# Regrouping the attention work between the steps of a feed-forward stage: four head pairs in one phase, one phase per step

## The chip, the core and the metric

The kernel runs on one core of a Trainium2 chip. The core has TensorE (PE: matrix products, whose weight loads are shown as PEld), VectorE (DVE), ScalarE (ACT), GpSimd (POOL) and SyncE (SP, which here only issues transfers). Each engine works through its own instruction stream in order; semaphores join them. The metric is the device time of one execution in microseconds, the median of several runs.

## The reference

Two stages follow each other: a linear-attention recurrence over 768 time steps, for 4 batches and 8 heads of width 48, and a feed-forward stage over the 3072 resulting rows of width 384.

```python
for t in range(S):                                    # B, H, S, D = 4, 8, 768, 48
    kt, vt, rt, wt = (k[:, :, t], v[:, :, t], r[:, :, t], w[:, :, t])
    cur = np.einsum('bhd,bhe->bhde', u[None] * kt, vt)
    y[:, :, t] = np.einsum('bhd,bhde->bhe', rt, state + cur)
    state = wt[:, :, :, None] * state + np.einsum('bhd,bhe->bhde', kt, vt)
...
x = attn_out.transpose(0, 2, 1, 3).reshape(B * S, H * D)
h = x @ w_in                                          # 384 x 2048
g = h - np.tanh(h)
return (g @ w_out).astype(np.float32)                 # 2048 x 384
```

All inputs but the weights are float32. The two weight matrices arrive as 64-bit floats and are turned into 32-bit ones on the chip, from their two 32-bit halves.

## The kernel before

**Blocks.** The work is cut into 8 blocks (4 batches, 2 stretches of 384 time steps, `NB`). A block's attention yields `xT`, the transposed 384 x 384 input of its feed-forward stage. That stage has 16 steps (`NF`): step `f` multiplies `xT` with 128 columns of w_in into `hp` (`first`, L374), ScalarE and VectorE form g from it (six operations L381 to L386, five L389 to L396), and two steps later (`LAG`) g is multiplied with w_out and added up in three accumulators `acc` (`Second.add`, L410). The attention of block i+1 runs between the steps of block i; block 0's attention runs ahead of everything ("boot"), and the last block's steps have none beside them. After the last step three tiles `o` are copied from `acc` and stored (L414, L416).

**Attention.** 64 time steps form a chunk, and two heads, one on partitions 0 to 47 and one on 64 to 111, form a pair. `scores` holds, for each pair of time steps of a chunk, how much of the later one's result comes from the earlier one. It is filled level by level: a first product of `kmix` and `rmix` (L222, masked into `scores` at L229), and then for m = 2, 4, 8, 16, 32 a product of `kq` and `rp` of half the width (masked in at L239; for 32 copied by ScalarE at L245). Between the levels `rp` and `kq` are multiplied by products of the decays w: rp on VectorE (L257), kq on GpSimd (L259), and the products `tot` themselves are formed on VectorE (L262). Then kq is transposed (L279, copied to `ks` at L281), multiplied with v (L296), and VectorE carries the states through the chunks (L303). Last come the products of rp with the states (L317) and, behind a fence, of v with the scores (L333), copied to `xT` by ScalarE (L344); the fourth pair goes to `late`, from which six small transfers fill the free partitions of `xT` (L352).

**What sets the order.** A `unit` is a generator that does this for two of the four pairs (`UP = 2`), and yields after each piece. A block has two units (g = 0, 1) that take turns, 20 pieces in all. The main loop asks for `PHASES * NG * (f + 1) / (NF - 1)` pieces by step f, so one step has one piece and the next may have two. TensorE's stream follows the program; those of the other engines are ordered by the scheduler from its own costs. All attention products use one PSUM tile `att` (pool `ps_a`, one buffer of two banks), so a piece's products wait until the products before have been read. Input tiles are double-buffered (`inp`, `once`), v_sb too.

**Weights.** `load_weights(f)` turns one tile of 128 x 768 weights: ScalarE takes the low half (`up`, L164) and the magnitude of the high half (L165), VectorE clamps (L166), takes the sign (L168), shifts (L169) and combines (L171), and GpSimd adds `up` (L173) as 32-bit integers. Three tiles are turned in boot, the others during block 0.

Of the kernel before, what the change touches and what calls it, by code (L numbers as in the profile page):

```python
# [34 lines left out]
F32 = mybir.dt.float32  # L36
# [10 lines left out]
P = 128  # L47
# [7 lines left out]
NG = NPAIR // UP  # L55
# [8 lines left out]
PHASES = 10  # L64
# [11 lines left out]
LOWEST = float(np.array(896 << 20, np.int32).view(np.float32))  # L76
HIGHEST = float(np.array(1151 << 20, np.int32).view(np.float32))
# [3 lines left out]
def kernel(  # L81
# [13 lines left out]
    inp = ctx.enter_context(tc.tile_pool(name="inp", bufs=2))  # L95
    once = ctx.enter_context(tc.tile_pool(name="once", bufs=2))
# [32 lines left out]
    for m in (2, 4, 8, 16):  # L129
        make_mask(m, m, 0)  # L130
# [3 lines left out]
    scores = []  # L134


    states = []
    for i in range(2):
        a = const.tile([P, 2, UP, NCP, L], F32, name=f"scores{i}", tag=f"scores{i}")
        nc.vector.memset(a, 0.0)  # L140
        scores.append(a)
    for g in range(NG):
        row = []
        for q in range(NQ):
            st = const.tile([P, UP, NCH, L], F32, name=f"states{g}{q}", tag=f"states{g}{q}")
            nc.gpsimd.memset(st, 0.0)
            row.append(st)
        states.append(row)
# [3 lines left out]
    w_out_sb = w_sb[:, :, DM:2 * DM]  # L152

# [3 lines left out]
    def load_weights(f):  # L157
        raw = conv.tile([P, 2 * DM, 2], I32, name="raw", tag="raw")
        nc.gpsimd.dma_start(out=raw, in_=weights[f].bitcast(I32).rearrange("p (n two) -> p n two", two=2))
        lo, hi = raw[:, :, 0], raw[:, :, 1]  # L160
        a = conv.tile([P, 2 * DM], I32, name="a", tag="a")
        sign = conv.tile([P, 2 * DM], I32, name="sign", tag="sign")
# [5 lines left out]
        nc.vector.tensor_single_scalar(sign, hi, -2 ** 31, op=ALU.bitwise_and)  # L168
        nc.vector.tensor_scalar(out=a, in0=a, scalar1=1 << 27, scalar2=4,  # L169
                                op0=ALU.bitwise_xor, op1=ALU.logical_shift_left)  # L170
        nc.vector.scalar_tensor_tensor(out=a, in0=a, scalar=1, in1=sign,  # L171
                                       op0=ALU.logical_shift_right, op1=ALU.bitwise_or)
        nc.gpsimd.tensor_tensor(out=w_sb[:, f, :].bitcast(I32), in0=a, in1=up, op=ALU.add)  # L173
# [4 lines left out]
    def unit(b, q, g, ps, v_sb, xT, late):  # L178


        A, St = scores[g], states[g][q]
        cols = slice(q * NB, (q + 1) * NB)
        pairs = slice(UP * g, UP * (g + 1))

        def load(pool, name, src):
            t = pool.tile([P, UC], F32, name=name, tag=name)
            nc.sync.dma_start(out=t.rearrange("d (p t) -> d p t", p=UP),
                              in_=src[b, pairs, :, cols].rearrange("p d t -> d p t"))
            return t


        rmix = load(once, "rmix", rT)
        kmix = load(once, "kmix", kT)
        rp = load(inp, "rp", rT)
        kq = load(inp, "kq", kT)
        wt = load(inp, "wt", wT)
        for p in range(UP):
            for t, odd in ((rmix, 0), (kmix, 1)):
                part = t[:, p * NB:(p + 1) * NB].rearrange("d (n two) -> d n two", two=2)[:, :, odd]
                nc.scalar.activation(out=part, in_=part, func=AF.Copy,  # L200
                                     scale=u_sb[:, UP * g + p:UP * g + p + 1])

        def new_ps():
            return ps.tile([P, 2, BANK], F32, name="att", tag="att")

        def gram(lhs, rhs, m, width):

            n = NCP * UP * width
            ps_t = new_ps()
            gr = ps_t[:, :, 0:n].rearrange("s h (p c t) -> s h p c t", p=UP, c=NCP)  # L210
            for p in range(UP):
                for c in range(NCP):
                    for h in range(2):
                        for par in range(2):
# [3 lines left out]
                            dst = gr[64 * par:64 * par + 64, h, p, c, :]  # L218
# [5 lines left out]
            return ps_t[:, :, 0:n]  # L224

        def take(gr, m):
            if m == 1:
                mask = masks[1].bitcast(U8).rearrange("s b j -> s (b j)").unsqueeze(1).unsqueeze(1)
                nc.vector.copy_predicated(  # L229
                    out=A.rearrange("s h p c t -> s h (p c) t"),  # L230
                    mask=mask.to_broadcast([P, 2, UP * NCP, L]),
                    data=gr.rearrange("s h (n t) -> s h n t", t=L))
                return
            nb = L // (2 * m)
            for h in range(2):
                dst = A[:, h].rearrange("s p c (b two m) -> s (p c) b two m", two=2, m=m)[:, :, :, 1, :]
                src = gr[:, h].rearrange("s (n b m) -> s n b m", b=nb, m=m)
                mask = masks[m].bitcast(U8).unsqueeze(1).to_broadcast([P, UP * NCP, nb, m])
                nc.vector.copy_predicated(out=dst, mask=mask, data=src)  # L239

        def take_top(gr):

            for par in range(2):
                rows = slice(64 * par, 64 * par + 32)
                nc.scalar.copy(out=A[rows].rearrange("s h p c t -> s h (p c) t")[:, :, :, 32:],  # L245
                               in_=gr[rows].rearrange("s h (n t) -> s h n t", t=32))

        take(gram(kmix, rmix, 1, L), 1)
        tot = wt
        m = 1  # L250
        while True:
            nblk = UC // (2 * m)
            t2 = tot.rearrange("d (n two) -> d n two", two=2)
            left, right = t2[:, :, 0], t2[:, :, 1]
            rv = rp.rearrange("d (n two m) -> d n two m", two=2, m=m)[:, :, 1, :]
            kv = kq.rearrange("d (n two m) -> d n two m", two=2, m=m)[:, :, 0, :]
            nc.vector.tensor_tensor(out=rv, in0=rv, op=ALU.mult,  # L257
                                    in1=left.unsqueeze(2).to_broadcast([P, nblk, m]))
            nc.gpsimd.tensor_tensor(out=kv, in0=kv, op=ALU.mult,  # L259
                                    in1=right.unsqueeze(2).to_broadcast([P, nblk, m]))  # L260
            nxt = work.tile([P, nblk], F32, name=f"tot{2 * m}", tag=f"tot{2 * m}")
            nc.vector.tensor_tensor(out=nxt, in0=left, in1=right, op=ALU.mult)  # L262
            tot = nxt
            m *= 2
            yield
            if m == L:
                break
            gr = gram(kq, rp, m, L // 2)
            if m == L // 2:
                take_top(gr)  # L270
            else:
                take(gr, m)


        ks = work.tile([P, UP, NCP, P], F32, name="ks", tag="ks")
        tp = new_ps()
        for p in range(UP):
            for c in range(NCP):
                nc.tensor.transpose(tp[:, p, c * P:(c + 1) * P],  # L279
                                    kq[:, p * NB + c * P:p * NB + (c + 1) * P], ident)  # L280
        nc.scalar.copy(out=ks.rearrange("t p c d -> t p (c d)"), in_=tp[:, :, 0:NCP * P])  # L281
        yield


        last = q == NQ - 1
        kvp = new_ps()
        for p in range(UP):
            for c in range(NCP):
                for h in range(2):
                    for par in range(2):  # L290
                        if last and 2 * c + par == NCH - 1:
                            continue
                        toks = slice(64 * par, 64 * par + 64)
                        e0 = (UP * g + p) * D2 + h * D
                        n0 = (p * NCP + c) * D
                        nc.tensor.matmul(kvp[64 * h:64 * h + 64, par, n0:n0 + D],  # L296
                                         lhsT=ks[toks, p, c, 64 * h:64 * h + 64],
                                         rhs=v_sb[toks, c, e0:e0 + D], start=True, stop=True)
        for c in range(NCH - 1 if last else NCH):
            for p in range(UP):  # L300
                dst = St[:, p, c + 1, 0:D] if c + 1 < NCH else states[g][q + 1][:, p, 0, 0:D]
# [192 lines left out]
```

## Time and profile before

| | us |
|---|---|
| median of 3 runs (904.54 to 908.07) | 907.02 |
| the profiled execution | 905.4 |
| its span, first to last instruction | 903.7 |
| TensorE busy | 736.0 (81%) |
| VectorE busy | 585.3 (65%) |
| ScalarE busy | 474.0 (52%) |
| GpSimd busy | 145.3 (16%) |
| matrix products of the feed-forward stage (acc, hp), busy | 322.5 + 278.4 |
| mean granted clock of TensorE, as a share of full speed | 0.923 |

Line numbers (L222) are those of the listing above. "a<-b,c" reads: a is written from b and c. Every float32 product appears as two records, so a step's six products are 12 records, and a piece of 24 products has 48. A wait is put down to what released it last. A TensorE record's duration includes some of the next one's time, as the products overlap; starts are the better clock.

### The profile page before, as it was taken

What the parts mean: (1) busy time and instruction counts of PE and PEld (TensorE: products, weight loads), DVE (VectorE), ACT (ScalarE), POOL (GpSimd) and SP (SyncE); (2) the same over time, 40 slices, a digit from 0 to 9 for tenths busy, and PEclk for the clock granted to TensorE, in tenths of its full rate; (3) what the DMA queues carried; (4) which work ended last, traced back from release to release, by engine and by line L of the source; (5) the groups of instructions that cost most, each with busy time, mean ns of one, the idle gap of its engine ahead of it and who ended that gap; (6) DMA issues with size and microseconds to landing.
All of it is one profiled execution on the core that took longest, in us unless ns stands there. A gap on an engine that the chain in (4) does not pass through costs nothing.

```text
span 903.7 us, 20566 instructions
## 1 busy us (share of the span) xinstructions
PE 736.0 (81%) x8480; PEld 458.7 (51%) x8480; DVE 585.3 (65%) x1221; ACT 474.0 (52%) x969; POOL 145.3 (16%) x163
## 2 busy tenths in 40 slices
PE   1664768888888888887888888888888888798997
PEld 1652445545555555554555555555555555455554
DVE  2999999647764576647746466554766466654674
ACT  2437356555464644546355453646545454545775
POOL 6555334001110011101110011100111001100000
PEclk9986789999999999999999888999999999999999
DMA  9476221140012300232011310113001100000000
GB/s 330 147 240 211 73 78 61 39 136 28 2 36 76 117 10 1 54 86 97 2 36 37 103 63 1 36 54 122 27 2 36 37 33 1 1 1 7 27 0 27
DMA packets 32493, 55.98 MB, mean 62 GB/s; under 512 B 2960, under 2 KB 30352, under 8 KB 32400
## 3 DMA queue, kind: packets, MB, share of 16 engines
q1 hardware_dynamic: 30096, 42.09, 14.8%
q0 software_dynamic: 2304, 12.58, 3.9%
q8 instruction: 67, 1.10, 0.5%
q14 instruction: 26, 0.21, 0.1%
HBM read 48.76 MB, written 4.72 MB: 59 GB/s over the span
## 4 chain that ended last, share of the span: by engine, by line
PE 58%; DVE 16%; ACT 12%; issue 5%; SPq 2%; DMA 2%; PEld 0%; PEldq 0%; DVEq 0%; ACTq 0%
PE acc L410 27%; PE hp L374 22%; PE att L222 5%; DVE hs L389 4%; PE att L317 3%; ACT s L382 3%; ACT h L381 3%; SPq L352 2%; DVE scores L239 2%; DVE hs L391 2%; DVE states L303 2%; DMA xT<-late 1%; ACT qa L383 1%; DVE gT L396 1%; ACT qb L384 1%
## 5 line engine op out<-in xcount | busy, mean ns | idle before, releaser
L410 PE MATMUL acc<-w_sb,gT 128*128 128x384 f32 x768 | 322.5, 563 | 1.3 <-ACT o L414 1.1
L374 PE MATMUL hp<-xT,w_sb 128*128 128x384 f32 x768 | 278.4, 496 | 9.7 <-DMA xT<-late 9.7
L389 DVE SCALAR_TENSOR_TENSOR hs<-h,s 128x384 f32<-128x384 f32 x128 | 106.5, 832 | 213.1 <-ACT s L382 212.8
L381 ACT COPY h<-hp 128x384 f32<-128x384 f32 x128 | 61.3, 479 | 343.9 <-PE hp L374 343.9
L374 PEld LDWEIGHTS hp<-xT,w_sb 128*128 128x128 f32 x768 | 150.7, 198 | 124.9 <-issue 22.4
L410 PEld LDWEIGHTS acc<-w_sb,gT 128*128 128x128 f32 x768 | 154.1, 212 | 98.0 <-issue 29.2
L259 POOL TENSOR_TENSOR kq<-kq,tot 128x384 f32<-128x384 f32 x80 | 74.2, 927 | 538.2 <-PE att L222 496.4
L222 PE MATMUL att<-rp,kq 48*64 48x32 f32 x3840 | 79.5, 232 | 66.5 <-DVE scores L239 54.9
L222 PEld LDWEIGHTS att<-rp,kq 48*64 48x64 f32 x3840 | 71.4, 148 | 98.9 <-issue 96.1
L396 DVE COPY_PREDICATED gT<-big,th 128x384 f32<-128x384 int32 x128 | 76.8, 600 | 7.4 <-DVE scores L239 0.2
L383 ACT ACTIVATE qa<-s,shift 128x384 f32<-128x384 f32 x128 | 76.9, 601 | 0.0
L384 ACT ACTIVATE qb<-s,shift 128x384 f32<-128x384 f32 x128 | 76.8, 600 | 0.0
L386 ACT ACTIVATE big<-s,shift 128x384 f32<-128x384 f32 x128 | 76.8, 600 | 0.0
L395 DVE TENSOR_TENSOR th<-h,th 128x384 f32<-128x384 f32 x128 | 76.7, 599 | 0.0
L393 DVE SCALAR_TENSOR_TENSOR gT<-qb,hs 128x384 f32<-128x384 f32 x128 | 71.6, 559 | 7.5 <-ACT big L386 0.5
L391 DVE SCALAR_TENSOR_TENSOR hs<-qa,hs 128x384 f32<-128x384 f32 x128 | 70.5, 550 | 0.0
L382 ACT ACTIVATE s<-h 128x384 f32<-128x384 f32 x128 | 66.8, 522 | 3.8
L239 DVE COPY_PREDICATED scores<-mask,att 128x192 f32<-128x192 uint8 x128 | 49.1, 410 | 26.3 <-PE att L222 26.1
L385 ACT ACTIVATE th<-h 128x384 f32<-128x384 f32 x128 | 64.9, 507 | 0.0
L317 PE MATMUL att<-rp,states 48*64 48x64 f32 x768 | 31.9, 246 | 20.0 <-ACT xT L344 19.6
L257 DVE TENSOR_TENSOR rp<-rp,tot 128x384 f32<-128x384 f32 x80 | 48.1, 601 | 0.0
L222 PE MATMUL att<-rmix,kmix 48*64 48x64 f32 x768 | 18.1, 252 | 32.9 <-DVE scores L229 21.1
(42 smaller groups left out, 460.2 us busy)
## 6 DMA issues: line engine op xcount, KB each, us to landing
raw<-in_weights POOLq DMA_DIRECT2D x16, 768.0 KB, 4.6
rmix<-in_rT SPq DMA_DIRECT2D x16, 384.0 KB, 3.3
kmix<-in_kT SPq DMA_DIRECT2D x16, 384.0 KB, 4.0
rp<-in_rT SPq DMA_DIRECT2D x16, 384.0 KB, 3.1
kq<-in_kT SPq DMA_DIRECT2D x16, 384.0 KB, 3.2
wt<-in_wT SPq DMA_DIRECT2D x16, 384.0 KB, 3.2
v_sb<-in_v SPq DMA_DIRECT2D x8, 576.0 KB, 4.0
out_y<-o SPq DMA_DIRECT2D x24, 192.0 KB, 1.9
```

The lines of the kernel that those rows point to most:

```text
L222: nc.tensor.matmul(dst, lhsT=lhs[rows, t0:t0 + L], rhs=src, start=True, stop=True)
L374: nc.tensor.matmul(hp, lhsT=w_in_sb[:, f, kc, :], rhs=xT[:, kc, :], start=(kc == 0), stop=(kc == KC - 1))
L381: nc.scalar.copy(out=h, in_=hp)
L382: nc.scalar.activation(out=s, in_=h, func=AF.Square)
L383: nc.scalar.activation(out=qa, in_=s, func=AF.Square, bias=shift[:, 0:1])
L384: nc.scalar.activation(out=qb, in_=s, func=AF.Square, bias=shift[:, 1:2])
L386: nc.scalar.activation(out=big, in_=s, func=AF.Relu, bias=shift[:, 2:3])
L389: nc.vector.scalar_tensor_tensor(out=hs, in0=h, scalar=SERIES, in1=s, op0=ALU.mult, op1=ALU.mult)
L391: nc.vector.scalar_tensor_tensor(out=hs, in0=qa, scalar=QUAD[0][1], in1=hs, op0=ALU.add, op1=ALU.mult)
L395: nc.vector.tensor_tensor(out=th, in0=h, in1=th, op=ALU.subtract)
L396: nc.vector.copy_predicated(out=g, mask=big.bitcast(I32), data=th)
L410: nc.tensor.matmul(acc, lhsT=g[:, j * P:(j + 1) * P], rhs=w_out_sb[:, f, :], start=(f == 0), stop=(f == NF - 1))
```

## The change

- The class `Block` takes the place of `unit`. Tiles hold all four pairs, twice as wide, and are single (`inp`, bufs=1); they are loaded by `load_all`, asked for at step 14 of the block before the one in whose steps they are used, so each load waits for the tile's last reader.
- A score phase handles all four pairs in one product group (48 products in one `att` tile); the first level and what follows the levels stay in halves. That makes 14 phases (`PHASES`), and the main loop takes one per feed-forward step, f = 0 to 13. The result's two product groups stand together in one phase.
- The multiplications of kq stand on VectorE (`decay`), not on GpSimd.
- Weights: ScalarE scales the magnitude by 2**-48 as it takes it, so that VectorE's shift left by 3 does what the exclusive-or and two shifts did; VectorE also adds `up`, and combines the sign straight into w_sb. GpSimd only issues the loads. Five tiles are turned in boot, one more per step after.
- Boot (`start`) loads k, r, w once per half, takes rmix and kmix from them (VectorE copies half of each, ScalarE scales the other half), and makes four masks and zeroes the states after the first products.
- The stores of out_y are issued by ScalarE, not SP.

```diff
-        nc.scalar.activation(out=a.bitcast(F32), in_=hi.bitcast(F32), func=AF.Abs)
+        nc.scalar.activation(out=a.bitcast(F32), in_=hi.bitcast(F32), func=AF.Abs, scale=SCALE)
...
-        nc.vector.tensor_single_scalar(sign, hi, -2 ** 31, op=ALU.bitwise_and)
-        nc.vector.tensor_scalar(out=a, in0=a, scalar1=1 << 27, scalar2=4,
-                                op0=ALU.bitwise_xor, op1=ALU.logical_shift_left)
-        nc.vector.scalar_tensor_tensor(out=a, in0=a, scalar=1, in1=sign,
-                                       op0=ALU.logical_shift_right, op1=ALU.bitwise_or)
-        nc.gpsimd.tensor_tensor(out=w_sb[:, f, :].bitcast(I32), in0=a, in1=up, op=ALU.add)
+        nc.vector.tensor_single_scalar(a, a, 3, op=ALU.logical_shift_left)
+        nc.vector.tensor_tensor(out=a, in0=a, in1=up, op=ALU.add)
+        nc.vector.scalar_tensor_tensor(out=w_sb[:, f, :].bitcast(I32), in0=hi, scalar=-2 ** 31, in1=a,
+                                       op0=ALU.bitwise_and, op1=ALU.bitwise_or)
...
+        def decay(self, m, p0, n):
+            cols = slice(p0 * NB, (p0 + n) * NB)
+            tot = self.tiles["wt"][:, cols] if m == 1 else self.tots[m, p0]
...
+            for t, half, by in ((self.tiles["kq"], 0, right), (self.tiles["rp"], 1, left)):
+                part = t[:, cols].rearrange("d (n two m) -> d n two m", two=2, m=m)[:, :, half, :]
+                nc.vector.tensor_tensor(out=part, in0=part, op=ALU.mult,
+                                        in1=by.unsqueeze(2).to_broadcast([P, nblk, m]))
...
+        def load_all(self):
+            for name, src in (("rmix", rT), ("kmix", kT), ("wt", wT), ("kq", kT), ("rp", rT)):
+                self.load(name, src, 0, NPAIR)
+            self.load_v()
+        def phases(self, ps):
+            self.mix(0, NPAIR, False)
+            for p0 in (0, UP):
+                self.level_1(ps, p0)
+                yield
+            m = 1
+            while m < L:
+                self.decay(m, 0, NPAIR)
+                m *= 2
+                if m < L:
+                    self.level(ps, m, 0, NPAIR)
+                    yield
+            for p0 in (0, UP):
+                self.turn(ps, p0)
+                yield
+                self.update(ps, p0, True)
+                yield
+            for p0 in (0, UP):
+                self.result(ps, p0)
+                yield
+            self.fill_holes()
+            yield
...
-                    nc.sync.dma_start(out=out[r0:r0 + P, :], in_=o)
+                    nc.scalar.dma_start(out=out[r0:r0 + P, :], in_=o)
...
-                while done < PHASES * NG * (f + 1) / (NF - 1):
-                    done += 1
-                    if next(run, True):
-                        break
+                next(run, None)
+                if f == PHASES and i + 2 < len(blocks):
+                    blocks[i + 2].load_all()
```

TensorE's stream before, within the score levels of a block (one line is a group of equal products; x24 is one unit's half block, x48 two of them in a row). Two steps with one piece, and one with two:

```order
L374 MATMUL hp<-xT,w_sb 128x384 x3
L222 MATMUL att<-rp,kq 64x32 x24
L410 MATMUL acc_2188<-w_sb,gT 128x384
L410 MATMUL acc_2189<-w_sb,gT 128x384
L410 MATMUL acc_2190<-w_sb,gT 128x384
L374 MATMUL hp<-xT,w_sb 128x384 x3
L222 MATMUL att<-rp,kq 64x32 x48
L410 MATMUL acc_2188<-w_sb,gT 128x384
```

The same place after:

```order
L414 MATMUL hp<-xT,w_sb 128x384 x3
L220 MATMUL att<-rp,kq 64x32 x48
L450 MATMUL acc_2068<-w_sb,gT 128x384
L450 MATMUL acc_2069<-w_sb,gT 128x384
L450 MATMUL acc_2070<-w_sb,gT 128x384
L414 MATMUL hp<-xT,w_sb 128x384 x3
L220 MATMUL att<-rp,kq 64x32 x48
L450 MATMUL acc_2068<-w_sb,gT 128x384
```

Before, an x48 row is two groups that write `att` one after the other; after, it is one group in one `att` tile, and every level's step looks alike.

VectorE's stream before, around one step of the levels (hs, th, gT are the dense operations; scores the masked copies; rp the products):

```order
L389 SCALAR_TENSOR_TENSOR hs<-h,s 128x384
L395 TENSOR_TENSOR th<-h,th 128x384
L239 COPY_PREDICATED scores_120<-mask_102,att 128x48x4
L391 SCALAR_TENSOR_TENSOR hs<-qa,hs 128x384
L239 COPY_PREDICATED scores_120<-mask_102,att 128x48x4
L393 SCALAR_TENSOR_TENSOR gT<-qb,hs 128x384
L257 TENSOR_TENSOR rp<-rp,tot_3154 128x96x4
L396 COPY_PREDICATED gT<-big,th 128x384
```

And after, at the level m = 16:

```order
L429 SCALAR_TENSOR_TENSOR hs<-h,s 128x384
L435 TENSOR_TENSOR th<-h,th 128x384
L431 SCALAR_TENSOR_TENSOR hs<-qa,hs 128x384
L263 COPY_PREDICATED scores<-mask_200,att 128x24x16
L433 SCALAR_TENSOR_TENSOR gT<-qb,hs 128x384
L263 COPY_PREDICATED scores<-mask_200,att 128x24x16
L436 COPY_PREDICATED gT<-big,th 128x384
L241 TENSOR_TENSOR kq<-kq,tot_0_4_2261 128x48x16
L241 TENSOR_TENSOR rp<-rp,tot_0_4_2261 128x48x16
```

The copies and products are twice as wide, and the two products of the next level stand behind all five dense operations of the step.

SP's stream after, for one block (before, each of rmix, kmix, kq, rp and wt had two loads of half the width, and the six fills stood behind the loads of wt and v too):

```order
L175 DMA wt<-in_wT 128x4x384
L175 DMA rmix<-in_rT 128x4x384
L175 DMA kmix<-in_kT 128x4x384
L175 DMA kq<-in_kT 128x4x384
L175 DMA rp<-in_rT 128x4x384
L182 DMA v_sb<-in_v 128x3x384
L347 DMA xT<-late 16x384 x6
```

The next block's wt now stands behind the fills, and rp and v ahead of them.

More of the change, by code (lines that the diff above doesn't have):

```diff
@@ L128 @@
     make_mask(1, 2, 1)
[L129 to L148, printed above, removed]
+    A = const.tile([P, 2, NPAIR, NCP, L], F32, name="scores", tag="scores")
+    nc.vector.memset(A, 0.0)
+    states = [const.tile([P, NPAIR, NCH, L], F32, name=f"states{q}", tag=f"states{q}")
+              for q in range(NQ)]
     w_sb = const.tile([P, NF, 2 * DM], F32, name="w_sb", tag="w_sb")
@@ L176 @@
-    fence, fences = tc.alloc_semaphore("fence"), []
[L178 to L211, printed above, removed]
@@ L241, in take_top, with level_1 @@
[L241 to L252, printed above, removed]
+            return used
+        def level_1(self, ps, p0):
+            gr = self.gram(ps, self.tiles["kmix"], self.tiles["rmix"], p0, UP, 1, L)
+            mask = masks[1].bitcast(U8).rearrange("s b j -> s (b j)").unsqueeze(1).unsqueeze(1)
+            nc.vector.copy_predicated(
+                out=A[:, :, p0:p0 + UP].rearrange("s h p c t -> s h (p c) t"),
+                mask=mask.to_broadcast([P, 2, UP * NCP, L]),
+                data=gr.rearrange("s h (n t) -> s h n t", t=L))
@@ L275, in unit @@
[L275 to L298, printed above, removed]
```

303 lines of the change are left out of this document (185 added, 118 removed).

## The prediction

> **What bounds the kernel now.** I read the busy times by stage first: block 0, one block in the middle, and the last one, cut where TensorE starts the first `hp` product of a block (columns: stretch, PE, PEld, DVE, ACT, POOL busy, granted clock, DMA share, GB/s).
>
> ```profile
> 64.20:191.20 127.00, 94.21 (x1041) 58.20 (x1042) 108.80 (x192) 69.17 (x132) 41.53 (x33) 0.82 0.31 101
> 191.20:297.30 106.10, 90.22 (x1069) 55.37 (x1068) 65.25 (x147) 55.71 (x118) 11.46 (x12) 0.94 0.17 51
> 830.10:903.70 73.60, 66.88 (x205) 38.23 (x203) 44.32 (x84) 50.71 (x105) 0.00 (x0) 0.99 0.05 18
> ```
>
> Three regimes: 64.2 us of boot attention, a block 0 in which VectorE is busy 109 of 127 us (it converts weights), six steady blocks of (830.1-191.2)/6 = 106.5 us in which TensorE is the busiest but idles 15.9 us each and has a granted clock of 0.94, and a last block of 73.6 us without attention. Then the waits of TensorE (us in total, times, longest):
>
> ```profile
> PE att L222 <- DVE scores L239: 54.9, 16, 6.9
> PE att L279 <- ACT ks L281: 22.2, 7, 3.2
> PE att L222 <- DVE scores L229: 21.1, 7, 7.6
> PE att L317 <- ACT xT L344: 19.6, 7, 2.8
> PE hp L374 <- DMA xT<-late: 9.7, 9, 6.2
> PE att L296 <- DVE states L303: 5.3, 7, 1.2
> ```
>
> All but the hole fills (xT<-late) and the state updates happen where two attention units follow each other in one feed-forward step and share the one `att` buffer: the second waits until DVE or ACT has read the first one's products. The timeline of PE shows what each costs (start, duration, idle before):
>
> ```profile
> 415.74 0.90 PE L222 MATMUL att<-rp,kq 48*64 48x32 f32 x48
> 416.57 2.20 PE L410 MATMUL acc<-w_sb,gT 128*128 128x384 f32 x6
> 418.62 2.10 PE L374 MATMUL hp<-xT,w_sb 128*128 128x384 f32 x6
> 420.64 0.90 PE L222 MATMUL att<-rp,kq 48*64 48x32 f32 x48
> ...
> 429.59 0.90 PE L222 MATMUL att<-rp,kq 48*64 48x32 f32 x48 [3.14 <-DVE scores L239]
> 430.42 3.90 PE L410 MATMUL acc<-w_sb,gT 128*128 128x384 f32 x6
> ...
> 481.03 0.92 PE L296 MATMUL att<-v_sb,ks 64*64 64x48 f32 x48 [1.18 <-DVE states L303]
> 481.87 2.20 PE L410 MATMUL acc<-w_sb,gT 128*128 128x384 f32 x6
> ```
>
> A step with one unit takes 420.64-415.74 = 4.90 us. With two it adds a 3.14 us wait, and then the `acc` products take 3.90 us where 2.20 is usual: the wait costs another 1.7 us, because the clock is halved afterwards, as this window shows; after a wait of 1.18 us it is not.
>
> ```profile
> 431.00:433.00 2.00, 2.00 (x5) 1.09 (x4) 1.56 (x5) 0.00 (x0) 0.61 (x1) 0.50 0.02 4
> ```
>
> Second, VectorE stands still behind GpSimd: an operation that takes 0.55 us takes 2.16 us when it starts inside GpSimd's weight addition, and `hs` 1.25 us inside a `kq` product.
>
> ```profile
> 58.51 0.95 DVE L171 SCALAR_TENSOR_TENSOR a<-a,sign 128x768 int32<-128x768 int32 x1
> ...
> 59.38 0.55 DVE L168 TENSOR_SCALAR sign<-raw 128x768 int32<-128x768 int32 x1
> 59.54 2.05 POOL L173 TENSOR_TENSOR w_sb<-a,up 128x768 int32<-128x768 int32 x1 [5.96 <-DVE a L171]
> ...
> 59.85 2.16 DVE L169 TENSOR_SCALAR a<-a 128x768 int32<-128x768 int32 x1
> ...
> 426.61 0.95 POOL L259 TENSOR_TENSOR kq<-kq,tot 128x384 f32<-128x384 f32 x1 [3.88 <-PE att L222]
> 426.72 1.25 DVE L389 SCALAR_TENSOR_TENSOR hs<-h,s 128x384 f32<-128x384 f32 x1
> ```
>
> **The change, part by part: a steady block.** A block multiplies the same records as before; only their places change. So its floor can be read from the block of before: 106.1 us, less 15.9 idle, less 6% of 106 for the clock, 83.8 us.
>
> What waits remain? Now one unit stands in each step, and in five steps it has 96 records instead of 48; 48 take 416.57-415.74 = 0.83 us, so these steps take 4.90+0.83 = 5.73 us on TensorE. Between two score units VectorE must do the first one's copies and the next level's products, and it is in-order, so the dense operations stand there too. Its spacing:
>
> ```profile
> 406.06 0.48 ACT L381 COPY h<-hp 128x384 f32<-128x384 f32 x1 [1.71 <-PE hp L374]
> ...
> 407.12 0.56 DVE L389 SCALAR_TENSOR_TENSOR hs<-h,s 128x384 f32<-128x384 f32 x1 [1.80 <-ACT s L382]
> 407.60 0.55 DVE L395 TENSOR_TENSOR th<-h,th 128x384 f32<-128x384 f32 x1
> 408.07 1.00 DVE L229 COPY_PREDICATED scores<-mask,att 128x768 f32<-128x768 uint8 x1
> 408.97 0.54 DVE L391 SCALAR_TENSOR_TENSOR hs<-qa,hs 128x384 f32<-128x384 f32 x1
> 409.61 0.56 DVE L393 SCALAR_TENSOR_TENSOR gT<-qb,hs 128x384 f32<-128x384 f32 x1
> ```
>
> An independent operation of 384 elements takes 0.47 us from start to start, one that needs the result just ahead 0.65, one of 768 elements 0.90. The new chain in a level step is hs 0.48, th 0.47, hs 0.65, gT 0.47, copy 0.5, gT copy 0.48, copy 0.5 (384 elements now), kq 0.87, rp 0.97 with its end: 5.4 us, starting 1.06+0.1 us after `hp` ends. So the next score unit can start 6.6 us after that end, where TensorE is ready after 5.73: the first level waits 0.9 us, and after that TensorE is itself late by as much and the chain of 5.4 fits into 5.73. Moving the k products to VectorE adds 0.87 us to this chain; TensorE covers it, and if a step were shorter than 5.6 us it would cost its excess in each level. The products `tot` of the next block stand in the last three steps, where VectorE has little else.
>
> Other waits. Seven of the eight scalings of rmix and kmix now stand together on ScalarE ahead of the fourth step's `h`:
>
> ```profile
> 410.28 0.83 ACT L200 ACTIVATE rmix<-rmix,u_sb 128x192 f32<-128x192 f32 x2 [1.26 <-DMA rmix<-in_rT]
> ```
>
> 8 x 0.83/2 = 3.3 us, of which ScalarE's slack (55.7 us busy in the block) should take about 1; the third and fourth steps then come 2.5 us later between them. The unit after each state update still waits for it: 5.3/7 = 0.75, twice, 1.5. The hole fills keep their 0.4 ((9.7-6.2)/8). Transposes and results no longer follow each other: nothing. Sum 5.3, and 1.0 for a halved clock after one wait in two blocks. A steady block comes to 83.8+5.3+1.0 = 90 us, 16.5 less, six times: **-99 us**.
>
> The Trainium skill ("TensorE: Matmul & The Clock Gate", Part 1) lets the clock fall only after an idle window of about 3.4 us; here a wait of 3.14 us was enough, and by the page no wait that I expect would cost clock: the sum would be 6 us lower.
>
> **Input loads.** The tiles are single now and twice as wide; SP is in order, and behind the last result unit (13th step) stand the loads of rp and v, the six hole fills and the next wt.
>
> ```profile
> raw<-in_weights POOLq DMA_DIRECT2D x16, 768.0 KB, 4.6
> 59.63 3.76 SPq L352 DMA_DIRECT2D xT<-late  x6
> ```
>
> 768 KB land in 4.6 us. From the end of that unit: about 1.1 us for ScalarE's copies, 3.8 for the fills, 4.6 for wt, so 9.5 us. VectorE reaches the products that need it in the 15th step, two steps of 420.64-416.57 = 4.1 us later, and 1.2 for ScalarE and 1.6 for three dense operations more: 11 us. Hidden, with a margin of 1.5 us; past it VectorE would hold dense results that TensorE needs two steps on. out_y moves from SP to ScalarE: three issues a block, bounded by the 0.6 us that each fill took SP (3.76/6) and by nothing; inside ScalarE's slack.
>
> **Boot and block 0.** Here VectorE is the bound. By the spacing of the rows above, a one-input operation of 768 elements takes 59.85-59.38 = 0.47 us and the combine 59.38-58.51 = 0.87. Per weight tile that is now clamp, sign and shift at 0.47 and the combine, 2.3 us, plus up to 2.05 behind GpSimd's addition, say 1.6. Afterwards: clamp, shift, an integer addition that no row shows on VectorE, and the combine. The addition costs between 0.87, the two-input operation of this width, and GpSimd's 2.05; I take 1.0, as the nearest row is of the same engine. 2.8 against 3.9 us: 16 x 1.1 = 17 us. The kq products cost 12 x 0.47 in boot and 6 x 0.87 in block 0, 11 us, and their blocking of `hs` and others, 0.7 at most in each of 24 (1.25-0.56), say 0.5, goes: nothing on balance. Boot gains four copies on VectorE, 2 us, and drops four loads of 384 KB ahead of its second half; I set 1 us of cost for both. VectorE is busy 86% of the time: **-14 us** of (17 - 1), with ends of -22 (2.05 us of blocking now, addition 0.87: (26.7-1) x 0.86) and +6 (1.2 of blocking now, addition 2.05: (5.8+1) x 0.86). The last block does not change.
>
> The skill's "VectorE: DVE Perf Modes" (perf-mode tier table) lets a two-input operation on 16-bit elements run at two per cycle; the addition is built as 128x1536 such elements, by which, with the page's 151 fixed cycles at 0.96 GHz, I estimate 0.96 us. No run here shows it.
>
> **Sum.** The profiled execution took 905.4 us, 0.2% under the median of 907.02. 905.4 - 99 - 14 = 792.4; against the median 0.2% more, **794 us**.
>
> **Rivals.** (a) The new chain decides: if gram, copies and products don't overlap with the dense work as I lined them up, each of five level steps waits 1.5 us and two waits a block halve the clock: 83.8 + 7.5 + 3.4 + 3 = 97.7, six times 9 gained: 905.4 - 54 - 14 = 838 us. For it speaks that VectorE would be busy some 75 us in a 90 us block and is in order; against it that the chain is 0.3 us shorter than a step.
> (b) The other side, slower: the single-buffered loads. The last reader of rp is the last result unit; were rp, v, fills and wt to land one after the other, each slowed by the others, DVE would hold the dense work behind `tot`, and TensorE would stop and lose its clock. The cover is three steps, 12 us; slower than before from 12+19 = 31 us of landing, as 113/6 = 19 is gained in a block. At 35 us: about 930 us. The 4.6 us above and 50 GB/s in the middle speak against it.
> (c) It does not do what it says: the waits only move from the `att` buffer to the products, 3 us at each of five levels with the clock halved behind each (5 x 4.7 = 23.5 us a block, as much as the 15.9 and 6.4 of now): within 0.5% of now, or 892 us with the start's 14. Its rows are those of (a).
>
> **Chances.** My forecast 0.68 (its own range 770 to 820), (a) 0.23, (b) 0.05, (c) 0.04. The range takes in (a) and the ends of the unknowns: low, block 86 us (no clock lost, 1.5 us of slack better used) and -22 for the start, 760; high, (a) without the start's gain, 852. About 0.5% either way is what a measurement of this kernel can tell from no change. Faster 0.93, same 0.02, slower 0.05.
>
> **What would show it.** The waits on the score copies (L239, L229) and on ks and xT for the `att` buffer fall from 118 us to under 25; steady blocks last 90 us with a clock above 0.97; no GpSimd work after the first 20 us but DMA issues, and `hs` at 0.56 us throughout; the addition at about 1 us; block 0 near 115 us. I am wrong if TensorE waits for `kq` or `rp` at every level, if DVE waits for `wt` in the 15th step, or if the clock stays at 0.94.

## The result, and the profile after

| | us |
|---|---|
| before, median of 4 runs (904.54 to 910.86) | 907.55 |
| after, median of 4 runs (783.6 to 792.61) | 789.5 |
| after / before, 95% interval | 0.8691 [0.8629, 0.8752] |
| predicted (range) | 794 (760 to 852) |
| span of the profiled execution after; granted clock | 789.3; 0.949 |

The change takes 13% off, and the forecast is 4.5 us too high. That is better than its parts were, as errors of both signs cancelled. First the stages, cut as before where TensorE starts a block's first `hp` product: block 0, a block in the middle, the last steady block and the last block (columns: stretch, PE, PEld, DVE, ACT, POOL busy, granted clock, DMA share, GB/s).

```profile
57.00:168.00 111.00, 92.58 (x1041) 58.82 (x1042) 90.22 (x174) 69.02 (x130) 4.78 (x9) 0.83 0.37 121
260.50:352.30 91.80, 84.95 (x1053) 53.81 (x1052) 61.76 (x126) 55.25 (x116) 0.00 (x0) 0.96 0.19 59
629.50:716.80 87.30, 83.51 (x1054) 52.70 (x1053) 59.47 (x121) 52.57 (x108) 0.00 (x0) 0.98 0.03 10
716.80:789.30 72.50, 66.44 (x205) 38.35 (x203) 44.31 (x84) 50.65 (x105) 0.00 (x0) 0.99 0.05 17
```

Boot takes 57.0 us instead of 64.2, block 0 111 instead of 127, the six steady blocks (716.80-168.00)/6 = 91.5 on average instead of 106.5, the last block 72.5 instead of 73.6. From the spans, 903.7 to 789.3: 23.2 us come from boot and block 0, 90.1 from the steady blocks, 1.1 from the last. Five of the steady blocks last 91.6 to 93.0 us, and one, the last of them, 87.2; that difference turns out to be the main lesson.

TensorE's waits, the largest first (us in total, times, longest):

```profile
PE att L220 <- DVE rp L241: 44.0, 18, 7.4
PE att L315 <- DVE states L300: 9.2, 7, 2.3
...
PE att L272 <- DVE states L300: 6.7, 7, 2.3
PE hp L414 <- DVE a L156: 6.7, 1, 6.7
PE acc L450 <- ACT o L454: 5.3, 6, 1.1
PE hp L414 <- DMA xT<-late: 2.4, 1, 2.4
...
PE att L220 <- DVE scores L227: 0.6, 1, 0.6
```

The 6.7 us put down to `a` are a wait at the end of boot for the fills of xT: in run 1 below, whose boot is the same, it is 6.8 us and stands as a wait for `xT<-late`. The waits for score copies, ks and xT, 118 us before, are down to 2.4 (0.6 here and 1.8 for ks). In their place stand waits for `rp`, the level products on VectorE. In a steady block they come twice, and the first is the dear one (TensorE's timeline; start, duration, idle before):

```profile
276.29 0.91 PE L450 MATMUL acc<-w_sb,gT 128*128 128x384 f32 x2 [0.79 <-ACT o L454]
277.04 2.10 PE L414 MATMUL hp<-xT,w_sb 128*128 128x384 f32 x6
282.68 2.78 PE L220 MATMUL att<-rp,kq 48*64 48x32 f32 x96 [3.54 <-DVE rp L241]
285.39 3.94 PE L450 MATMUL acc<-w_sb,gT 128*128 128x384 f32 x6
...
297.62 1.60 PE L220 MATMUL att<-rp,kq 48*64 48x32 f32 x96 [0.75 <-DVE rp L241]
```

3.54 us of waiting, and behind it the products take 2.78 and 3.94 us where 1.60 and 2.20 are usual: 2.9 us more of halved clock. What made `rp` late stands on ScalarE, in the step before (ScalarE's rows first, then VectorE's):

```profile
270.95 0.82 ACTq L456 DMA_DIRECT2D out_y<-o  x2
272.52 0.48 ACT L421 COPY h<-hp 128x384 f32<-128x384 f32 x1 [1.23 <-PE hp L414]
275.76 0.48 ACT L454 COPY o<-acc 128x384 f32<-128x384 f32 x1 [2.76 <-DMA out_y<-o]
276.13 0.53 ACT L422 ACTIVATE s<-h 128x384 f32<-128x384 f32 x1
...
276.69 0.56 DVE L429 SCALAR_TENSOR_TENSOR hs<-h,s 128x384 f32<-128x384 f32 x1 [3.93 <-ACT s L422]
...
281.59 0.94 DVE L241 TENSOR_TENSOR rp<-rp,tot 128x768 f32<-128x768 f32 x1
```

The tile o has two buffers and a block makes three; the third copy waits 2.76 us until the first store has landed, 275.76-270.95 = 4.8 us after its issue. ScalarE is in order, so `s` waits, and so do VectorE's `hs` (3.93 us), all that is queued behind `hs`, and the next group's `rp`. The store is late since the loads of rmix and kmix were issued at 268.48 and 268.90, just ahead of it; in this window the transfer engines are full:

```profile
272.00:274.00 2.00, 2.00 (x99) 1.55 (x97) 0.60 (x1) 0.48 (x1) 0.00 (x0) 1.00 1.05 376
```

The steady block of 87.2 us is the one that loads nothing for a block after it; its first wait is 1.75 us, not 3.54. In the kernel before, these loads stood further from the stores (304.33 and 304.75 against 313.65 us in the block that starts at 297.3), and the store landed in 1.9 us.

### The profile page after: what moved, and what is told of

Same layout as the page of the kernel before. It is cut to its first block, busy times and chain, and to the rows that moved or that the text cites. A ratio compares the mean times of both kernels' runs of the same rounds, so it can differ in the third digit from the quotient of the medians.

```text
span 789.3 us, 20068 instructions
## 1 busy us (share of the span) xinstructions
PE 695.6 (88%) x8480; PEld 445.4 (56%) x8480; DVE 558.0 (71%) x1138; ACT 470.9 (60%) x955; POOL 18.8 (2%) x49
## 4 chain that ended last, share of the span: by engine, by line
PE 51%; DVE 14%; ACT 10%; issue 7%; DMA 6%; PEld 5%; PEldq 1%; SPq 0%; ACTq 0%; DVEq 0%
PE acc L450 23%; PE hp L414 20%; PE att L220 6%; DMA out_y<-o 3%; DVE states L300 3%; ACT s L422 2%; DVE gT L436 2%; DVE gT L433 2%; DVE hs L431 2%; ACT h L421 2%; PEld att L315 2%; DMA raw<-in_weights 2%; DVE rp L241 2%; PE att L272 1%; ACT qa L423 1%
## 5 line engine op out<-in xcount | busy, mean ns | idle before, releaser
L450 PE MATMUL acc<-w_sb,gT 128*128 128x384 f32 x768 | 294.1, 521 | 5.4 <-ACT o L454 5.3
L414 PE MATMUL hp<-xT,w_sb 128*128 128x384 f32 x768 | 272.2, 491 | 9.0 <-DVE a L156 6.7
L414 PEld LDWEIGHTS hp<-xT,w_sb 128*128 128x128 f32 x768 | 147.7, 193 | 113.5 <-issue 14.4
L450 PEld LDWEIGHTS acc<-w_sb,gT 128*128 128x128 f32 x768 | 145.4, 200 | 96.8 <-issue 11.6
L429 DVE SCALAR_TENSOR_TENSOR hs<-h,s 128x384 f32<-128x384 f32 x128 | 71.2, 556 | 163.1 <-ACT s L422 163.0
L435 DVE TENSOR_TENSOR th<-h,th 128x384 f32<-128x384 f32 x128 | 70.5, 551 | 0.0
L263 DVE COPY_PREDICATED scores<-mask,att 128x384 f32<-128x384 uint8 (+1 forms) x72 | 43.5, 617 | 5.7 <-PE att L220 5.5
L241 DVE TENSOR_TENSOR kq<-kq,tot 128x768 f32<-128x768 f32 (+1 forms) x45 | 38.7, 860 | 0.3 <-PE att L220 0.3
L241 DVE TENSOR_TENSOR rp<-rp,tot 128x768 f32<-128x768 f32 (+1 forms) x45 | 38.7, 860 | 0.0
L300 DVE SCALAR_TENSOR_TENSOR states<-states,tot,att 128x48 f32<-128x48 f32 x176 | 34.9, 256 | 2.2 <-PE att L290 2.2
L315 PE MATMUL att<-rp,states 48*64 48x64 f32 x768 | 28.0, 230 | 9.2 <-DVE states L300 9.2
```

The lines of the kernel that those rows point to most:

```text
L241: nc.vector.tensor_tensor(out=part, in0=part, op=ALU.mult, in1=by.unsqueeze(2).to_broadcast([P, nblk, m]))
L414: nc.tensor.matmul(hp, lhsT=w_in_sb[:, f, kc, :], rhs=xT[:, kc, :], start=(kc == 0), stop=(kc == KC - 1))
L450: nc.tensor.matmul(acc, lhsT=g[:, j * P:(j + 1) * P], rhs=w_out_sb[:, f, :], start=(f == 0), stop=(f == NF - 1))
```

## The experiments

Differences below are to the 789.5 us of the new kernel, and the runs of the kernel before beside each (905.6 to 907.7 us) say that the chips agree within 0.3%. Ratios are to the kernel before, with their 95% interval. Line numbers of edited kernels are a few lines off the listing's.

**1. A third buffer for o.**

```diff
-                    o = dense.tile([P, DM], F32, name="o", tag="o")
+                    o = dense.tile([P, DM], F32, name="o", tag="o", bufs=3)
```

> The new kernel with a third buffer for the output tile o. Theory A: in the steady blocks the third copy into o waits 2.8 us for the first store, which lands late beside the loads of rmix and kmix; s, hs and with them the next level's products queue behind it on ScalarE and VectorE. That wait goes, but the next thing on ScalarE is a scaling of rmix placed between h and s, and its load lands only some 5.5 us after its issue, so s gains 1.5 us, not 2.8: blocks of 90 us, about 781 us in all. If the store alone is to blame, the five blocks come down to the 87.2 us of the one that has no loads: 765 us. Rival B, the 3.3 us of scalings on ScalarE make the wait by their length: no change, 789 us.

765.65 us (0.8426 [0.8389, 0.8463]), 24 us less. Theory A held in its main part; its extra clause, that a load of rmix would take the store's place, did not: the scaling between h and s finds its data there. A steady block:

```profile
254.30:342.20 87.90, 83.36 (x1053) 52.77 (x1052) 61.98 (x127) 55.24 (x116) 0.00 (x0) 0.98 0.19 62
```

**2. and 3. The scalings of rmix and kmix placed apart, without and with the third buffer.** Two of them are pinned behind ScalarE's dense operations in each of four steps.

```diff
+                if i + 2 < len(blocks):
+                    if f == 2:
+                        blocks[i + 2].load_mix()
+                    if 4 <= f < 4 + NPAIR:
+                        blocks[i + 2].scale(f - 4)      # keep_in_program_order
```

> The new kernel with the scalings of rmix and kmix pinned two by two behind the dense operations of the steps f = 4 to 7, o still in two buffers; the loads start when they did. Theory A: the wait for the store (15 us in six blocks) stays, and with it TensorE's 3.5 us wait: 785 to 789 us. Rival B (the length of the scalings): the wait falls to the 1.75 us of the block without loads, 765 us.

790.0 us (0.8703 [0.8666, 0.8741]): no difference, as theory A had it.

> Both edits: a third o buffer, and the scalings pinned behind steps 4 to 7. Theory A: nothing on ScalarE waits for a transfer any more; all steady blocks last about 87 us as the one without loads does, 5 x 4.9 = 24 us less, 765 us, mean clock above 0.96. If neither store nor load is at fault (rival C: VectorE's own chain at the first half-width level, whose two copies take 0.8 us each instead of 0.47, makes it): 785 us or more.

765.89 us (0.8439 [0.841, 0.8468]): the same as the third buffer alone. Where the scalings stand changes nothing that these runs can tell, in either setting. ScalarE's waits without the third buffer:

```profile
ACT o L469 <- DMA out_y<-o: 15.3, 6, 3.2
```

**4. Two groups a step again.** Only the grouping of the level products is undone, and with it each masked copy is cut in two.

```diff
-                    self.level(ps, m, 0, NPAIR)
+                    for p0 in (0, UP):
+                        self.level(ps, m, p0, UP)
```

> The new kernel, but the product group of each level is issued as two groups of 24 products, one after the other in the same step, each in its own turn in the one att buffer; all else stays. Theory: the wait of the old kernel is back, in each of the five level steps (3.1 us, and 1.7 us of halved clock behind it): up to 24 us a block in seven blocks, so 880 to 955 us, with TensorE's waits for the score copies above 80 us in all. Rival: the gain came from wider operations and a free GpSimd, not from one group a step: below 820 us.

895.23 us (0.9851 [0.9806, 0.9897]), 106 us more: nearly the whole gain is gone with this one edit, while the wide tiles, the free GpSimd and the new boot stay. The steady blocks last 107.9 to 113.5 us, the last of them 102.7, and the old kind of wait is back, five times a block as before, though now at the five levels:

```profile
PE att L220 <- DVE scores L263: 82.2, 28, 4.7
PE att L220 <- ACT scores L255: 21.4, 7, 3.1
```

**5. kq's products on GpSimd again** (`nc.gpsimd` for half 0 in `decay`).

> The new kernel with the products of kq back on GpSimd. As the prediction had it: the balance of 0.87 us less VectorE work a level against 0.5 to 0.7 us of blocking is nothing, 785 to 795 us. Theory: worse than that, since at 768 elements GpSimd needs 1.8 us (twice the 0.95 of 384), the rp product beside it is held up, and so a level step's chain gets up to 1 us longer than with both on VectorE, at five levels in seven blocks and in boot: 800 to 830 us, with TensorE's waits for kq or rp above 44 us. Rival (the engines really work side by side): 39 us less work on VectorE, 770 to 780 us.

808.65 us (0.8914 [0.8884, 0.8944]), 19 us more. In the profiled execution 8.6 of them are in boot (65.6 us instead of 57.0) and 7.8 in the six steady blocks. What blocks whom in a steady block, VectorE first, then GpSimd:

```profile
209.62 1.91 DVE L432 SCALAR_TENSOR_TENSOR hs<-qa,hs 128x384 f32<-128x384 f32 x1
```

```profile
209.28 1.83 POOL L242 TENSOR_TENSOR kq<-kq,tot 128x768 f32<-128x768 f32 x1 [6.55 <-DVE hs L430]
```

An hs of 0.55 us ends 0.4 us after the GpSimd product that it started in. Against my expectation TensorE's waits for rp and kq did not grow (40 us in all); those for the states did, from 9.2 us to 16.1. Boot loses its time in another way. GpSimd also issues the weight loads, and the next of these loads stands behind block 1's kq product, which waits for its own input. ScalarE then waits for the weights, and the last copies of the attention's result, from which xT is filled, stand behind that wait:

```profile
50.38 2.93 POOL L242 TENSOR_TENSOR kq<-kq,wt 128x768 f32<-128x768 f32 x1 [8.25 <-DMA kq<-in_kT]
...
61.20 0.89 ACT L151 ACTIVATE a<-raw 128x768 f32<-128x768 f32 x1 [10.44 <-DMA raw<-in_weights]
```

TensorE's wait at the end of boot is 12.2 us, against 6.7 in the new kernel; the other 3.1 of the 8.6 us are lost ahead of it. The prediction had the move of kq as nothing on balance; it is a gain of the change.

**6. The weights' addition on GpSimd again** (`nc.gpsimd.tensor_tensor` for the addition alone).

> The new kernel with the integer addition of the weights back on GpSimd (shift and combine stay on VectorE, the shift two steps ahead of the combine). By the prediction's sum, VectorE has 0.87 us less work a tile and up to 2.05 us, 1.6 taken, of standing behind GpSimd: 16 x 0.73 x 0.86 = 10 us slower, 793 to 805 us, all of it before the first steady block. Rival (no standing behind GpSimd): 16 x 0.87 x 0.86 = 12 us faster, 777 us.

794.25 us (0.8751 [0.8717, 0.8785]), 4.8 us more, and the interval reaches into that of the new kernel. The sign is as expected; the size is half the 10 us of the sum, but the two intervals leave both nothing and 10 us open.

**7. The stores issued by SP again.**

```diff
-                    nc.scalar.dma_start(out=out[r0:r0 + P, :], in_=o)
+                    nc.sync.dma_start(out=out[r0:r0 + P, :], in_=o)
```

> The new kernel with the stores of out_y issued by SP, as the old kernel did; o keeps two buffers. Theory: the store is late because the loads of rmix and kmix fill the transfer engines, not because of the queue that issues it; ScalarE's wait for it stays near 15 us: 785 to 793 us. Rival (issuing on ScalarE is what costs): below 780 us.

774.78 us (0.8533 [0.8496, 0.857]), 15 us less: my theory failed, and moving the stores to ScalarE is a part of the change that costs time. But the rival's reason, that the issuing itself costs ScalarE its time, isn't it either: 9 keeps the issues on ScalarE and is faster still. On SP the two stores stand in line between the two loads:

```profile
262.40 0.37 SPq L175 DMA_DIRECT2D rmix<-in_rT  x1
264.87 0.83 SPq L456 DMA_DIRECT2D out_y<-o  x2
266.13 0.39 SPq L175 DMA_DIRECT2D kmix<-in_kT  x1
```

So only one load is ahead of them. The third copy, which here also stands behind s, starts 2.9 us after the first store's issue and waits for nothing:

```profile
267.35 0.51 ACT L422 ACTIVATE s<-h 128x384 f32<-128x384 f32 x1
267.76 0.46 ACT L454 COPY o<-acc 128x384 f32<-128x384 f32 x1
...
273.73 1.54 ACT L200 ACTIVATE kmix<-kmix,u_sb 128x192 f32<-128x192 f32 x4 [3.22 <-DMA kmix<-in_kT]
```

Instead a scaling waits 3.2 us for kmix, but behind the step's dense operations. The new place of the copy, behind s, is the smaller part of this: the first store here landed 2.68 us after its issue, and by that the copy in the new kernel, ready at 272.52+0.48 = 273.00, would have waited 270.95+2.68-273.00 = 0.6 us instead of 2.76 (an estimate).

**8. The third buffer, and VectorE's attention work ahead of the dense work that can wait.**

```diff
+                with tc.high_priority():
                     self.decay(m, 0, NPAIR)
...
+                    with tc.high_priority():
                         self.level(ps, m, 0, NPAIR)
```

> Three o buffers, and in the steady blocks the products of kq and rp and the masked copies placed on VectorE ahead of the dense operations that can wait (hs, gT), so that the next group's products start some 1.2 us earlier in each level step. Theory: what is left of TensorE's waits for rp in a steady block, 2.0 and 0.75 us, and the halved clock behind the first go, 4 us a block, 6 blocks, and some of the waits in block 0: 735 to 745 us, clock above 0.975. Rival (the dense results become late instead, TensorE waits for gT): 760 us or more.

753.47 us (0.8305 [0.8267, 0.8343]), 12 us less than the third buffer alone, but not the 735 to 745. Boot took 65.7 us instead of 57.0: with priority, VectorE has a product of block 1's decays in its queue ahead of boot's own, and block 1's wt had not landed. This wait is 3.3 of the 8.7 us; where the rest goes is open.

```profile
26.77 0.96 DVE L244 TENSOR_TENSOR tot<-wt 128x768 f32<-128x768 f32 x1 [3.30 <-DMA wt<-in_wT]
```

**9. The loads of rmix and kmix held back**, o in two buffers and the stores on ScalarE as in the new kernel. After the fifth level two one-column products read the old tiles, so that the loads must come later; the scalings are pinned behind steps 10 to 13 (pinning alone does nothing, 2).

```diff
+                    if m == 32:
+                        for n, x, y, c in (("jr", "rmix", "rp", 63), ("jk", "kmix", "kq", 0)):
+                            j = work.tile([P, 1], F32, name=n, tag=n)
+                            nc.vector.tensor_tensor(out=j, in0=self.tiles[x][:, 0:1],
+                                                    in1=self.tiles[y][:, c:c + 1], op=ALU.mult)
```

> The new kernel with o still in two buffers and its stores still issued by ScalarE, but the loads of rmix and kmix held back: two one-column products on VectorE after the fifth level read the old tiles, so the loads start some 20 us after the stores, and the scalings stand behind the steps f = 10 to 13. Theory: a store that has the transfer engines to itself lands in 1.9 us and the third copy into o waits for nothing; ScalarE's 15 us of waiting for stores fall below 2, and the time comes to that of the kernel with three o buffers, 762 to 772 us. Rival (the store is slow of itself, or by its queue): 785 us or more.

765.31 us (0.8418 [0.8374, 0.8462]): the same 24 us as with the third buffer. With the loads away, ScalarE starts the third copy 1.9 us after the first store's issue, without a wait:

```profile
260.11 0.82 ACTq L476 DMA_DIRECT2D out_y<-o  x2
...
262.05 0.48 ACT L474 COPY o<-acc 128x384 f32<-128x384 f32 x1
```

1 and 9 take the wait away in two independent ways and gain the same, so the cause is shown: two loads in flight ahead of a store that a two-buffer tile waits for.

**10. and 11. Priority where no load is waited for, and for the state updates too** (as 8, but `decay(1)` without priority, `update` with it); 11 also runs boot's second half first.

> Three o buffers; on VectorE the level products and masked copies go ahead of the dense work that can wait, but for the first level, whose inputs come from a load, and the state updates go ahead too. Theory: the kernel with every level ahead lost 9 us in boot, since VectorE stood in order behind products of block 1 whose loads had not landed; these 9 us come back, and TensorE's waits for the states (1.0 and 1.3 us a block, sometimes with a halved clock behind them) go: 753 - 9 - 6 x 1.5 = 735 us, between 728 and 745. Rival (the dense results become late, TensorE waits for gT): 750 us or more.

719.73 us (0.7921 [0.7877, 0.7966]), far below the 735: the best version, 21% under the kernel before. Boot 60.2, block 0 91.7, and the steady blocks 82.3 to 82.8 us with the clock at 1.00:

```profile
234.40:316.90 82.50, 81.43 (x1053) 51.90 (x1052) 63.68 (x129) 55.20 (x116) 0.00 (x0) 1.00 0.21 66
```

```profile
170.15 1.60 PE L220 MATMUL att<-rp,kq 48*64 48x32 f32 x96 [0.70 <-DVE scores L263]
```

Of TensorE's waits one of 0.5 to 0.9 us a steady block is left.

> The same, and boot handles its second half first from the transposes on, so that the tile late, from which the free partitions of xT are filled, is ready 3 us earlier. Theory: TensorE's wait for these fills at the start of block 0 (2.4 us in the new kernel, up to 9 in others) shrinks by 2 to 3 us: 730 to 735 us. Rival (the weights on VectorE are what block 0 waits for): as without it, within 2 us.

722.14 us (0.7954 [0.7907, 0.8001]): no gain; the intervals overlap. TensorE's wait for the fills of xT in boot fell from 9.2 to 6.8 us, but block 0 took 94.3 us instead of 91.7. What else boot waits for is left open.

**12. Two groups a step, with the order of 10.**

> The kernel with three o buffers and VectorE's order set for the attention work, but with each level's products again in two groups of 24 in one step that share the one att buffer. Theory: even when VectorE copies the first group as soon as it is there, TensorE waits for its last product, the semaphore and two copies of 0.3 us, some 1.1 us, at five levels in seven blocks: 38 us, and more where the clock is halved behind it: 755 to 790 us. Rival (the old waits came from VectorE's order alone, not from two groups in one buffer): below 735 us.

779.49 us (0.8598 [0.8558, 0.8637]), 60 us more than 10. As expected, in size too:

```profile
PE att L220 <- DVE scores L263: 39.0, 28, 1.5
PE att L220 <- ACT scores L255: 11.6, 7, 2.3
```

These two waits are 50.6 us, where 10 waits 5.3 us for the score copies, so most of the 60 us is waiting for the shared buffer. Two groups in one buffer cost 106 us with the order that the change left on VectorE and 60 us with the better one: sharing the buffer is the larger part of that loss, and VectorE's order made it worse. No run gave two groups a buffer each.

## Why the prediction was right, step by step

**One group a step.** Right, and shown by 4 and 12: this is most of what the change gains. The floor was 83.8 us; 10 comes to 82.5 with 1.07 idle (82.50-81.43), so it is 81.4. In the block at 260.50 the waits are 91.80-84.95 = 6.85 us where I had 5.3, and the halved clock costs 84.95-81.4 = 3.5 where I had 1.0. Sum 91.8 against 90.

**The stores on ScalarE: the step that failed.** "out_y moves from SP to ScalarE ... inside ScalarE's slack" priced the issues (0.82 us for two) and not the wait behind them. The move costs 15 us (7), and the wait for the store 24 (1, 9). I had the rows to see it: three copies, two buffers, and a load of 4.6 us next to them.

**The scalings.** I put 2.5 us a block on their length; 2 and 3, which spread them over four steps, change the time by less than 1 us. This term, 15 us in six blocks, hid more than half of the missing one; that the total still came out is luck to this extent.

**The first level.** I had 0.9 us of wait; in the block without the store's wait it is 1.75. My chain took 0.5 us for each masked copy of 384 elements; at m = 2, where a row's runs are two elements long, it takes twice that, and from m = 4 on it is as I took it:

```profile
277.17 1.01 DVE L263 COPY_PREDICATED scores<-mask,att 128x384 f32<-128x384 uint8 x1
...
285.52 0.57 DVE L263 COPY_PREDICATED scores<-mask,att 128x384 f32<-128x384 uint8 x1 [0.92 <-PE att L220]
```

Of the three groups behind that one waits, 0.75 us; elsewhere the chain fits, as I had it.

**State updates, hole fills, loads.** Two waits of 0.56 to 1.6 us for the states in a block: I had 0.75 each. The hole fills cost TensorE nothing after the start of block 0. The loads are hidden: VectorE waits 16 and 9 us in all for the next rp and kq, in steps where TensorE does not need it.

**Boot and block 0.** Predicted -14, measured -23.2. The addition was sized right, 1.0 against 0.95 us:

```profile
L156 DVE CUSTOM_DVE_ANT_0 a<-a,up 128x1536 uint16<-128x1536 uint16 x16 | 15.2, 950 | 0.1
```

The Trainium skill's "VectorE: DVE Perf Modes" (perf-mode tier table), from which I had estimated 0.96 us, agrees with the 0.95 of the trace. The term that was mis-sized is the kq products, "nothing on balance": put back on GpSimd they cost 9 us in boot and 1 in block 0 (5). I had weighed only their length and the blocking of VectorE; 5.5 of the 9 us come from the weight loads that stand behind them on GpSimd. The weights' own part may have been too large: the addition on GpSimd costs 4.8 us more than on VectorE (6) where the sum had 10, but the runs don't tell the two apart. I also gave block 0 no share in the regrouping of block 1's attention, which runs in its steps; undone in 4, block 0 takes 3.3 us more. How the rest of its 16 us divides was not tried.

**GpSimd.** As predicted it is idle in the steady blocks (0.00 in the windows above), and hs, 0.83 us on average before, is short throughout:

```profile
L429 DVE SCALAR_TENSOR_TENSOR hs<-h,s 128x384 f32<-128x384 f32 x128 | 71.2, 556 | 163.1 <-ACT s L422 163.0
```

**The clock.** Predicted above 0.97 in the steady blocks, it is 0.96 where the store is waited for and 0.98 where not. The Trainium skill ("TensorE: Matmul & The Clock Gate", Part 1) counts idle windows of about 3.4 us that run free of the kernel, and by it no wait of a steady block here but that of 3.5 us should cost clock. The trace does not agree on the length: 1.75 us were enough here, the last row at half the usual speed.

```profile
648.84 1.60 PE L220 MATMUL att<-rp,kq 48*64 48x32 f32 x96 [1.75 <-DVE rp L241]
650.37 3.86 PE L450 MATMUL acc<-w_sb,gT 128*128 128x384 f32 x6
```

**The rivals.** (a), that VectorE's chain decides, did not come at every level, but it names what was left: 8 and 10 shorten that chain by order alone and take 12 and 46 us off the third buffer's 765.65. (b) and (c) did not come.

## What to carry to other kernels

When a phase is regrouped, ask of each tile in the new place how many buffers it has against how many are made at a time, and which transfers are in flight when its store must land: a store that lands within 1.9 us alone holds an in-order engine, and everything behind it, when two loads are ahead of it. Two product groups that share one PSUM buffer within a step cost TensorE the wait for the copy between them and some clock; one wide group doesn't. On an in-order engine that serves two streams, put the work on which the next TensorE group waits ahead of the work that is due two steps later; here that was worth almost twice as much as the buffer. But don't put an operation that waits for a load in front: 8 lost time so on VectorE and 5 on GpSimd, each in boot.

## What the hardware showed that I had not expected

The queue that issues a transfer matters through its place in line: the same store had landed after at most 2.9 us on SP's queue, ahead of the second load (7), and took 4.8 us on ScalarE's, with both loads ahead. The Trainium skill's "DMA: Bandwidth & Descriptors" (Issuing engines are not separate DMA queues) says that transfers of all queues run on the same 16 engines and interleave. The trace agrees on the engines, with their share at 1.05 in the window above, and not on the interleaving. Of the new kernel's queues, SP's (q1, the loads) has all the packets from 272 to 274 us, the first row, though the first store was issued at 270.95; ScalarE's (q10, the stores) has its first packets in the next 2 us, the other rows (columns: packets, MB, share of 16 engines).

```profile
q1 hardware_dynamic: 505, 0.75, 105.4%
...
q10 hardware_dynamic: 287, 0.39, 52.9%
q1 hardware_dynamic: 136, 0.18, 26.1%
```

The store on another queue came after the loads nearly as if it stood in one line with them.

No fixed length of a wait halves the clock. In the new kernel 1.75 us for `rp` did (above). In 1 a wait of 1.79 us at the same place did not, and the `acc` behind it keeps its 2.20 us:

```profile
627.77 1.60 PE L220 MATMUL att<-rp,kq 48*64 48x32 f32 x96 [1.79 <-DVE rp L241]
629.30 2.20 PE L450 MATMUL acc<-w_sb,gT 128*128 128x384 f32 x6
```

In the kernel before, TensorE waited 3.17 us for ks in each of seven blocks; six times the `acc` behind kept its speed, as here, and once it took 3.53 us:

```profile
258.30 0.85 PE L279 MATMUL att<-ident,kq 128*128 128x128 f32 x6 [3.17 <-ACT ks L281]
258.98 2.10 PE L410 MATMUL acc<-w_sb,gT 128*128 128x384 f32 x6
```

So the 1.7 us that the prediction read behind a wait of 3.14 us is a frequent price and not a sure one. In 12 even a wait of 1.23 us was followed by half the speed, in two of six blocks:

```profile
260.02 1.11 PE L220 MATMUL att<-rp,kq 48*64 48x32 f32 x48 [1.23 <-DVE scores L263]
261.06 3.63 PE L454 MATMUL acc<-w_sb,gT 128*128 128x384 f32 x6
```
